# The opening of a routed-attention and tanh-shrink kernel: order of weight fetches, first masks and a later pair's loads

## The chip, the cores and the metric

One core of one Trainium2 chip. The metric is device microseconds of one execution. The kernel before the change takes 991.08 us (median of 3 runs, 991.01 to 991.74). Engine names: TensorE (PE, its weight loads PEld), VectorE (DVE), ScalarE (ACT), GpSimd (POOL, "the pool"), and SyncE (SP), whose queue issues most of the DMAs.

## What is computed

Attention in which a query and a key see each other only if both have the same nearest centroid, and then a two-layer block over the joined heads. Batch 4, 8 heads, 768 positions, 64 channels per head, 16 centroids; the block goes from 512 to 2048 and back.

```python
q_assign = np.argmax(np.einsum('bhsd,hcd->bhsc', q_n, c_n), axis=-1)
k_assign = np.argmax(np.einsum('bhsd,hcd->bhsc', k_n, c_n), axis=-1)
mask = q_assign[:, :, :, None] == k_assign[:, :, None, :]
scores = np.where(mask, scale * np.matmul(q, k.transpose(0, 1, 3, 2)), -1e9)
attn = softmax(scores)                 # over the keys
x = np.matmul(attn, v)                 # heads joined: (3072, 512)
h = x @ w_in
out = (h - np.tanh(h)) @ w_out
```

The two weight matrices arrive as 8-byte floats and are read as pairs of 32-bit words; q, k and v are 4-byte floats.

## The kernel before

**Pairs and steps.** Two heads make a pair, so there are 16 pairs; pairs 0 to 3 (HP is 4) are batch 0. The scores of a pair are made transposed, keys on the partitions, in two halves of 384 queries, and each half in three steps of 256 keys. The list `steps` (L904) has 96 entries (pair, half, step): the first 12 are the first halves of pairs 0 to 3, the next 12 their second halves, then one pair after the other.

**One step.** `begin` (L435) makes the scores on TensorE (L443) and the exponentials on ScalarE (L465). `select` (L467) multiplies a tile of exponentials, on VectorE, by 1 where the key's code equals the query's code, else 0 (L475). It reads the queries' codes from a tile `row`, in which they are spread over all 128 partitions. `value` (L490) multiplies by v on TensorE (av, L497). `sum_up` (L504) adds up the denominators of the first halves on TensorE (den, L511 and L518). The loop from L1031 writes a step's work in this order: what belongs to later pairs, `begin` of the following step, `rest_of` for today's weight pieces, `value`, `sum_up`, then a list `todo` (select of the following step, stages of later pairs, denominators, weight pieces). The order is manual; each engine gets its instructions in the order in which the code writes them.

**Codes.** For each pair, `turn` (L319) transposes q and k (pt, L324; copied out by ScalarE, L331), `similar` (L337) multiplies by the centroids (sim, L343), `route` (L350) finds the best centroid with four VectorE operations (L362 to L369), and `publish` (L383) transposes the codes (pq, L388), copies them (qc, L392) and writes them to DRAM through SP (L394). From there `spread` (L398) loads a `row` (L401). In the first halves of pairs 1 to 3, `masked` (L378), no `select` is needed: `spread_both` (L406) loads the codes of both sides into a tile `hot` (L410), `one_hot` (L414) turns it into the two factors of a mask on VectorE (L418, L422), and `begin` adds the mask to the scores by matmuls (L454).

**Opening.** Lines 980 to 1019 are written out by hand: loads of pair 0 (`load`, L302, four DMAs on SP's queue for q and k, and two for v), constants, the codes of pair 0, its first `row`, the codes of pair 1, and `begin` of the steps 0, 1 and 2. The stages of the later pairs (`before`, L908: turns, similar, route, publish, spread_both, one_hot) are put on steps by a table (L927 to L935); for pair 3 they fall on steps 3, 4, 4, 5, 5 and 7. `turns` of pair 3 also calls `load(4)`, which has no buffer to wait for.

**Weight pieces.** The matrices come in 32 pieces of 512 KB, fetched by the pool's queue (`fetch`, L209, DMA at L217) into three buffers. `rest_of` (L219) makes two ScalarE operations of a piece (L148, L149), into one of two buffers `rest`; `round_piece` (L224) makes two VectorE operations (L157, L160) and then fetches the piece three further on. Pieces are counted from 0 here. Pieces 0 and 1 are done in the opening, where a small pool copy, the gate (L987), holds back the first fetches until pair 0's k has come. The table `paces` (L1028) says how many pieces each step takes.

**Denominators of the first halves.** For pairs 0 and 1, `total`, `compact`, `invert`, `spread_out` and `scale` (L530 to L585) follow at steps +0, +1, +2, +3 and +5 after a half's last step: SP writes a list (L550), loads it compactly (L563, tiles each and other), VectorE adds and inverts (L571, L572), SP writes it back (L574) and spreads it (den<-back, L579), VectorE scales (L585). Pairs 2 and 3 are divided directly (`divide`, L587).

From step 12 on the block of batch 0 fills the gaps (h at L612, o at L628), and later batches use a seven-product scheme (pu at L804, pd at L855).

Of the kernel before, what the change touches and what calls it, by code (L numbers as in the profile page):

```python
# [58 lines left out]
def kernel(  # L59
# [10 lines left out]
    nc = tc.nc  # L70
# [8 lines left out]
    HP = H // 2  # L79
# [98 lines left out]
    def fast():  # L178
# [123 lines left out]
        def load(n: int, what=(0, 1)):  # L302
            if n >= len(pairs):
                return
            b, p = pairs[n]
            for i in what:
                if i < 2:
                    pool, tag = (gp, "g") if b == 0 else (loads, f"x{i}")
                    t = raw_qk[n, i] = pool.tile([P, NCH, 2, D], F32, name=f"x{i}", tag=tag)
                else:  # L310
                    pool = vp0 if n in (2, 3) else vp
                    t = vals[n] = pool.tile([P, 2, NCH, D], F32, name="vals")
                for h in range(2):
                    nc.sync.dma_start(
                        t[:, :, h] if i < 2 else t[:, h],
                        (q, k, v)[i][b, 2 * p + h].rearrange("(p j) d -> p j d", p=P),
                    )

        def turn(n: int, i: int, engine):  # L319

            pt = ps_s.tile([P, 2, 512], F32, name="pt", tag="s")
            x = raw_qk.pop((n, i))
            for j in range(NCH):
                nc.tensor.transpose(  # L324
                    out=pt[:, j // HCH, (j % HCH) * P : (j % HCH + 1) * P],
                    in_=x[:, j].rearrange("p h d -> p (h d)"), identity=ident,
                )
            pool = turnp0 if n in (2, 3) else turnp
            t = turned[n, i] = pool.tile([P, 2, TB], F32, name=f"t{i}")
            if engine is nc.scalar:  # L330
                nc.scalar.copy(out=t, in_=pt[:, :, 0:TB])  # L331
            else:
                nc.vector.tensor_copy(out=t, in_=pt[:, :, 0:TB])
# [3 lines left out]
        def similar(n: int):  # L337

            ps = ps_f.tile([P, TB], F32, name="sim", tag="f")
            for i in range(2):  # L340
                for half in range(2):
                    r = (2 * i + half) * 2 * C
                    nc.tensor.matmul(  # L343
                        ps[r : r + 2 * C], lhsT=bd[:, pairs[n][1]],
                        rhs=turned[n, i][:, half], start=True, stop=True, tile_position=(0, r),
                    )
            sims[n] = rtp.tile([P, TB], F32, name="simt")
            nc.scalar.copy(out=sims[n], in_=ps)
# [25 lines left out]
        def summed(n: int, half: int):  # L374

            return n < HP and half == 0

        def masked(n: int, half: int):  # L378


            return summed(n, half) and n > 0
# [14 lines left out]
        rows, hots = {}, {}  # L396
# [9 lines left out]
        def spread_both(n: int):  # L406

            t = hots[n] = gp.tile([P, 2, 2, TB], BF16, name="hot", tag="g")
            for h in range(2):
                nc.sync.dma_start(  # L410
                    t[h * D : h * D + D], q_codes[n][:, :, h].unsqueeze(0).to_broadcast([D, 2, 2, TB])
                )
# [16 lines left out]
        def weight_tiles(n: int, half: int, s: int):  # L429
            if (n, half, s) == (0, 0, NS - 1):  # L430
                return [gp.tile([P, 2, TB], F32, name="e", tag="g") for _ in range(2)]
            t = ep.tile([P, 2, 2, TB], F32, name="e")
            return [t[:, i] for i in range(2)]

        def begin(step):  # L435
            n, half, s = step
            sc = {}
            for i in range(2):
                j = 2 * s + i
                sc[i] = ps_s.tile([P, 2, 512], F32, name="sc", tag="s")  # L440
                for h in range(2):
                    r = slice(h * D, h * D + D)
                    nc.tensor.matmul(  # L443
                        sc[i][:, h, 0:TB],
                        lhsT=turned[n, 1][r].rearrange("p a n -> p (a n)")[:, j * P : (j + 1) * P],
                        rhs=turned[n, 0][r, half], start=True, stop=not masked(n, half),
                    )
            for i in range(2):
                j = 2 * s + i
                out = sc[i][:, :, 0:TB]  # L450
                if masked(n, half):
                    for h in range(2):
                        r = slice(h * D, h * D + D)
                        nc.tensor.matmul(  # L454
                            sc[i][:, h, 0:TB],
                            lhsT=hots[n][r, 1].rearrange("p a n -> p (a n)")[:, j * P : (j + 1) * P],
                            rhs=hots[n][r, 0, half], start=False, stop=True,
                        )
                if summed(n, half):
                    if i == 0:  # L460
                        weights[n, half, s] = weight_tiles(n, half, s)
                    out = weights[n, half, s][i]
                else:
                    scores[n, half, j] = sc[i]
                nc.scalar.activation(out=out, in_=sc[i][:, :, 0:TB], func=ACT.Exp, scale=SCALE)  # L465

        def select(n: int, half: int, j: int):  # L467

            if not masked(n, half):
                if j % 2 == 0 and not summed(n, half):  # L470
                    weights[n, half, j // 2] = weight_tiles(n, half, j // 2)
                e = weights[n, half, j // 2][j % 2]
                sc = e if summed(n, half) else scores.pop((n, half, j))
                for h in range(2):
                    nc.vector.scalar_tensor_tensor(  # L475
                        out=e[:, h], in0=rows[n, half][:, h],
                        scalar=codes[n][:, 1, j // HCH, h, j % HCH : j % HCH + 1], in1=sc[:, h, 0:TB],
                        op0=ALU.is_equal, op1=ALU.mult,
                    )
            if j % 2 == 1 and not summed(n, half):  # L480
                pair = weights[n, half, j // 2]
                if j == 1:
                    s = sums[n, half] = sump.tile([P, 2, TB], F32, name="sum")
                    nc.gpsimd.tensor_tensor(out=s, in0=pair[0], in1=pair[1], op=ALU.add)  # L484
                else:
                    s = sums[n, half]
                    for i in range(2):
                        nc.gpsimd.tensor_tensor(out=s, in0=s, in1=pair[i], op=ALU.add)  # L488
# [278 lines left out]
        def strassen_items(b: int):  # L767
# [136 lines left out]
        steps = [(p, half, s) for half in range(2) for p in range(HP) for s in range(NS)] + [  # L904
            (n, half, s) for n in range(HP, len(pairs)) for half in range(2) for s in range(NS)
        ]

        def before(n: int):  # L908


            def turns():
                turn(n, 0, nc.scalar)
                turn(n, 1, nc.scalar)
                if n >= HP - 1:
                    load(n + 1)

            yield turns
            yield lambda: similar(n)
            yield lambda: route(n)
            yield lambda: publish(n)  # L920
            if masked(n, 0):
                yield lambda: spread_both(n)
                yield lambda: one_hot(n)


# [60 lines left out]
        gate = const.tile([P, 1], F32, name="gate")  # L986
# [16 lines left out]
        load(2)  # L1003
        rest_of(1)
        begin(steps[0])
        for _ in range(2):
            round_piece(rounding.pop(0))
        route(1)
        begin(steps[1])
        begin(steps[2])  # L1010
        publish(1)
        spread_both(1)
        load(1, (2,))
        load(3)
        for n in range(2, HP):
            load(n, (2,))
        for i in range(2):
            select(*steps[0][:2], i)
        ready[1] = {**ready.get(1, {}), 5: lambda: one_hot(1)}


# [3 lines left out]

        paces = dict(enumerate((0, 0, 1, 2, 0, 0, 2, 2, 1, 1, 1, 0, 3, 2, 2, 2, 2, 2, 2, 3, 2)))  # L1028
        late, divides, makers, later = [], [], [], {}
        fill, whole, spent, since, over = [], 0.0, 0.0, 0, 1  # L1030
        for at, (n, half, s) in enumerate(steps):  # L1031
# [108 lines left out]
        for t, bound in (  # L1140
# [7 lines left out]
            out=fits, in0=inverse, scalar1=MOST_INVERSE * words, scalar2=None, op0=ALU.is_le  # L1148
        )
        nc.vector.scalar_tensor_tensor(  # L1150
            out=fits, in0=inverse, scalar=words / SUM_MOST, in1=fits, op0=ALU.is_ge, op1=ALU.mult
        )
        checks = [fits, largest]
        if words == 2:
            nc.vector.tensor_scalar(
                out=smallest, in0=smallest, scalar1=HIGH_LEAST, scalar2=None, op0=ALU.is_ge
# [161 lines left out]
    with ExitStack() as cx, tc.manual_schedule():  # L1318
        fast()
# [35 lines left out]
```

## Time and profile before

| | value |
|---|---|
| median of 3 runs | 991.08 us |
| span of the profiled execution | 990.3 us (that run: 992.06 us) |
| granted TensorE clock | 0.998 |
| VectorE busy | 531.4 us |
| ScalarE busy | 321.7 us |
| pool busy | 499.7 us |
| DMA moved | 132.47 MB, mean 134 GB/s |

A line of the chain of waits has a start and a duration in us, and what ran: an engine and its line, a DMA, or "issue", time in which the engine waited for nothing that the profile shows. A line of the timeline has a start, a duration, engine, line, operation, written tile <- read tiles, shapes and a count; in brackets stands how long the engine was idle before it and what ended that. "SPq" is SP's queue. Windows give each engine's busy time in a stretch, and what share of the 16 DMA engines was busy.

### The profile page before, as it was taken

How to read it: one execution, taken by the hardware profiler on the slowest of the kernel's cores; microseconds unless marked ns; L12 is line 12 of the kernel's file. 1: busy time of each engine (PE TensorE's matmuls, PEld its weight loads, DVE VectorE, ACT ScalarE, POOL GpSimd, SP SyncE). 2: the span in 40 equal slices, each digit the busy share in tenths (PEclk: the TensorE clock that was granted, in tenths of full speed). 3: DMA queues.
4: the chain of work that ended last, by engine and by line, in shares of the span. 5: the costliest groups of instructions: out<-in, count | busy, mean ns of one | idle time of the engine just before them, and what ended most of it. 6: DMA issues, size and time to landing. Idle time of an engine off the chain costs nothing.

```text
span 990.3 us, 16579 instructions
## 1 busy us (share of the span) xinstructions
PE 976.6 (99%) x6444; PEld 467.0 (47%) x6444; DVE 531.4 (54%) x1017; ACT 321.7 (32%) x493; POOL 499.7 (50%) x346
## 2 busy tenths in 40 slices
PE   7999999999999999999999999999999999999997
PEld 4344443344443334444455555444455555444664
DVE  5547567448655667656554357655645336533011
ACT  5566564233442333343331222324341221122000
POOL 1015334444445464786777345676688345466600
PEclk9999999999999999999999999999999999999999
DMA  8854363125475724463536637344453232233321
GB/s 209 211 136 140 112 181 105 30 51 153 120 217 144 218 91 126 147 173 118 176 111 201 193 117 215 109 148 123 149 166 95 99 110 74 103 112 127 103 102 35
DMA packets 115977, 132.47 MB, mean 134 GB/s; under 512 B 62980, under 2 KB 95668, under 8 KB 113204
## 3 DMA queue, kind: packets, MB, share of 16 engines
q1 hardware_dynamic: 109508, 109.81, 37.3%
q0 software_dynamic: 6240, 21.50, 6.6%
q8 instruction: 53, 0.87, 0.4%
q14 instruction: 32, 0.26, 0.1%
q10 hardware_dynamic: 144, 0.03, 0.0%
HBM read 110.14 MB, written 21.17 MB: 133 GB/s over the span
## 4 chain that ended last, share of the span: by engine, by line
PE 96%; DVE 2%; DMA 1%; ACT 1%; issue 0%; POOL 0%; ACTq 0%; DVEq 0%
PE pd L855 22%; PE pu L804 21%; PE sc L443 14%; PE av L497 14%; PE o L628 8%; PE h L612 8%; PE pt L324 2%; PE den L537 2%; PE sim L343 1%; PE warm L294 1%; PE den L511 1%; DMA row<-q_codes 1%; PE pr L356 1%; DVE e L475 1%; PE den L518 0%
## 5 line engine op out<-in xcount | busy, mean ns | idle before, releaser
L488 POOL TENSOR_TENSOR sum<-sum,e 128x768 f32<-128x768 f32 x112 | 206.1, 1840 | 107.6 <-DVE e L475 103.8
L475 DVE SCALAR_TENSOR_TENSOR e<-row,code,sc 128x384 f32<-128x384 bf16 x336 | 185.2, 607 | 99.1 <-ACT sc L465 77.8
L855 PE MATMUL pd<-stream,G 128*64 128x256 f32 x1728 | 191.8, 379 | 0.0
L465 ACT ACTIVATE sc<-sc 128x768 f32<-128x768 f32 x168 | 125.9, 792 | 202.7 <-PE sc L443 187.9
L855 PEld LDWEIGHTS pd<-stream,G 128*64 128x64 f32 x1728 | 123.8, 137 | 67.4 <-issue 7.9
L443 PE MATMUL sc<-t,t 64*128 64x384 f32 x768 | 150.0, 509 | 0.9 <-ACT e L465 0.9
L497 PE MATMUL av<-e,vals 128*64 128x384 f32 x768 | 145.6, 498 | 1.8 <-DVE e L475 1.8
L799 POOL TENSOR_TENSOR G<-G,th 128x768 f32<-128x768 f32 (+1 forms) x51 | 88.0, 1738 | 98.6 <-ACT th L797 98.6
L804 PE MATMUL pu<-xT,stream 128*64 128x384 f32 x768 | 134.9, 488 | 0.7 <-DVE top L364 0.7
L804 PE MATMUL pu<-diff,stream 128*64 128x384 f32 x576 | 103.1, 487 | 0.0
L443 PEld LDWEIGHTS sc<-t,t 64*128 64x128 f32 x768 | 66.0, 186 | 74.8 <-issue 41.9
L484 POOL TENSOR_TENSOR sum<-e 128x768 f32<-128x768 f32 x28 | 56.8, 2028 | 74.6 <-DVE e L475 66.3
L804 PEld LDWEIGHTS pu<-xT,stream 128*64 128x64 f32 x768 | 54.1, 137 | 69.5 <-issue 62.5
L497 PEld LDWEIGHTS av<-e,vals 128*64 128x64 f32 x768 | 47.6, 136 | 83.1 <-issue 78.9
L612 PE MATMUL h<-xT,w_in 128*64 128x384 f32 x512 | 86.3, 487 | 0.1
L628 PE MATMUL o<-w_out,g 128*64 128x512 f32 x384 | 86.3, 594 | 0.0
L797 ACT ACTIVATE th<-G 128x768 f32<-128x768 f32 (+1 forms) x51 | 40.9, 806 | 117.6 <-DVE G L792 114.0
L804 PEld LDWEIGHTS pu<-diff,stream 128*64 128x64 f32 x576 | 40.8, 137 | 49.9 <-issue 44.5
L792 DVE TENSOR_TENSOR G<-pu,u 128x384 f32<-128x384 f32 x72 | 39.8, 552 | 41.4 <-PE pu L804 41.2
L612 PEld LDWEIGHTS h<-xT,w_in 128*64 128x64 f32 x512 | 36.4, 137 | 46.3 <-issue 44.7
L628 PEld LDWEIGHTS o<-w_out,g 128*64 128x64 f32 x384 | 27.1, 137 | 50.3 <-issue 49.6
L866 DVE SCALAR_TENSOR_TENSOR c<-pd,du 128x256 f32<-128x256 f32 x36 | 15.1, 420 | 62.5 <-PE pd L855 62.5
(123 smaller groups left out, 843.5 us busy)
## 6 DMA issues: line engine op xcount, KB each, us to landing
stream<-up_factors SPq DMA_DIRECT2D x24, 896.0 KB
stream<-down_factors SPq DMA_DIRECT2D x21, 1024.0 KB
raw<-in_moe_w_in_dram POOLq DMA_DIRECT2D x16, 512.0 KB, 5.8
raw<-in_moe_w_out_dram POOLq DMA_DIRECT2D x16, 512.0 KB, 5.2
again<-in_moe_w_in_dram SPq DMA_DIRECT2D x32, 256.0 KB
again<-in_moe_w_out_dram SPq DMA_DIRECT2D x32, 256.0 KB
x<-in_q_dram SPq DMA_DIRECT2D x32, 192.0 KB
x<-in_k_dram SPq DMA_DIRECT2D x32, 192.0 KB
```

Of the source, the lines that this page charges most:

```text
L443: nc.tensor.matmul(sc[i][:, h, 0:TB], lhsT=turned[n, 1][r].rearrange("p a n -> p (a n)")[:, j * P : (j + 1) * P], rhs=turned[n, 0][r, half ...
L465: nc.scalar.activation(out=out, in_=sc[i][:, :, 0:TB], func=ACT.Exp, scale=SCALE)
L475: nc.vector.scalar_tensor_tensor(out=e[:, h], in0=rows[n, half][:, h], scalar=codes[n][:, 1, j // HCH, h, j % HCH : j % HCH + 1], in1=sc[: ...
L484: nc.gpsimd.tensor_tensor(out=s, in0=pair[0], in1=pair[1], op=ALU.add)
L488: nc.gpsimd.tensor_tensor(out=s, in0=s, in1=pair[i], op=ALU.add)
L497: nc.tensor.matmul(avs[n, half][h * D : h * D + D], lhsT=vals[n][:, h, j], rhs=e[i][:, h], start=(j == 0), stop=(j == NCH - 1),)
L612: nc.tensor.matmul(h[r], lhsT=w_in[i][:, c, o * P : (o + 1) * P][:, r], rhs=xT[c][:, half], start=(c == 0), stop=(c == CD - 1),)
L628: nc.tensor.matmul(acc[sub][r], lhsT=gs[f % HF][:, f // HF, sub * P : (sub + 1) * P][:, r], rhs=w_out[f // FQ][:, f % FQ], start=(f == seq ...
L797: nc.scalar.activation(out=th, in_=t, func=ACT.Tanh)
L799: nc.gpsimd.tensor_tensor(out=t, in0=t, in1=th, op=ALU.subtract)
L804: nc.tensor.matmul(ps[r], lhsT=streams[base + i][:, c, k_, r], rhs=right[c], start=(c == 0), stop=(c == CH - 1),)
L855: nc.tensor.matmul(ps[r], lhsT=left(i)[:, r], rhs=t[:, i], start=(i == 0), stop=(i == HF - 1))
```

## The change

Four edits, all to the order of the work; what is computed stays.

```diff
@@ before(n): turns()
-                if n >= HP - 1:
+                if n >= HP:
                     load(n + 1)
@@ before(n)
             if masked(n, 0):
-                yield lambda: spread_both(n)
+
+                def spreads():
+                    spread_both(n)
+                    if n == HP - 1:
+                        load(n + 1)
+
+                yield spreads
                 yield lambda: one_hot(n)
@@ opening
         begin(steps[0])
+
+        nc.gpsimd.tensor_copy(out=gate, in_=rows[0, 0][:, 0, 0:1])
         for _ in range(2):
             round_piece(rounding.pop(0))
         route(1)
         begin(steps[1])
-        begin(steps[2])
+        select(*steps[0][:2], 0)
         publish(1)
         spread_both(1)
+        begin(steps[2])
         load(1, (2,))
         load(3)
         for n in range(2, HP):
             load(n, (2,))
-        for i in range(2):
-            select(*steps[0][:2], i)
+        select(*steps[0][:2], 1)
@@ paces
-        paces = dict(enumerate((0, 0, 1, 2, 0, 0, 2, 2, 1, 1, 1, 0, 3, 2, 2, 2, 2, 2, 2, 3, 2)))
+        paces = dict(enumerate((0, 0, 1, 1, 1, 0, 2, 2, 1, 1, 1, 0, 3, 2, 2, 2, 2, 2, 2, 3, 2)))
```

The load of pair 4's q and k goes from the step of pair 3's turns (step 3) to that of its `spread_both` (step 5). A second gate on the pool reads one element of each partition of the first `row`, ahead of the fetches of pieces 3 and 4 (the fourth and fifth). The first tile of step 0 is selected before the codes of pair 1 are published, and `begin` of step 2 comes after that. Step 3 takes one piece instead of two, and step 4 one instead of none.

## The prediction

> **What bounds the kernel now.** I read the page's busy shares first, then its chain that ended last.
>
> ```profile
> span 990.3 us, 16579 instructions
> PE 976.6 (99%) x6444; PEld 467.0 (47%) x6444; DVE 531.4 (54%) x1017; ACT 321.7 (32%) x493; POOL 499.7 (50%) x346
> PE 96%; DVE 2%; DMA 1%; ACT 1%; issue 0%; POOL 0%; ACTq 0%; DVEq 0%
> ```
>
> TensorE is busy all but 13.7 us, so a change that leaves its work alone wins only idle time. Windows of 25 us place it: 5.4 us idle in 0:25, 1.6 in 25:50, then 25.00 of 25 nearly everywhere (24.66 the lowest), and 5.9 in the last window, at the tail, which the change doesn't touch. So at most the 7.0 us of the opening are to be had. The chain in order of time, in 14:48, shows where they lie:
>
> ```profile
> 17.45 6.42 DMA row<-q_codes
> ...
> 23.96 0.63 DVE e L475
> 24.59 0.04 issue
> 24.63 2.45 PE av L497 x8
> 27.08 0.10 issue
> 27.18 0.85 PE pt L324 x6
> 28.03 0.47 issue
> 28.50 0.85 PE pt L324 x6
> ...
> 43.84 0.65 ACT t L331
> 44.49 0.04 issue
> 44.54 1.54 PE sim L343 x8
> 46.08 1.49 PE sc L443 x8
> ```
>
> Two places matter. First, the row broadcast takes 6.42 us; TensorE waits for the first select until 24.63, and the first eight av matmuls, 1.44 us elsewhere in the chain, take 2.45 at the DVE's pace. Second, sim of pair 3 waits for ScalarE's copy at 43.84, which stands behind two weight pieces. After 46 us nothing idles, but the timeline shows a tight place ahead, in VectorE and ScalarE rows of 61:72:
>
> ```profile
> 61.85 0.55 DVE L585 TENSOR_TENSOR xT<-xT,den 128x384 f32<-128x384 f32 x1
> 66.49 0.17 DVE L571 TENSOR_TENSOR each<-each,other 128x6 f32<-128x6 f32 x1 [4.08 <-DMA other<-list]
> 68.05 0.79 ACT L148 ACTIVATE rest<-raw 128x512 uint16<-128x512 uint32 x1 [0.90 <-DVE w_in L160]
> 70.18 1.51 ACT L465 ACTIVATE e<-sc 128x768 f32<-128x768 f32 x2
> ```
>
> VectorE waits 4.08 us for a small list; rest of piece 9 then waits for piece 7's buffer, and the exponentials of step 10 start at 70.18, right behind. TensorE needs the first of them at 72.96 (the scores of step 11).
>
> [...] 979 KB moved from 18 to 23 us, by the half-microsecond windows, while the row is 192 KB. [...] the second pair's codes, issued from 23.71, behind the 768 KB of pair 2's q and k, let the hot loads start only at 29.21.
>
> **The change part by part.** "Step" is an entry of the list of 96.
>
> *A. Pieces 3 and 4 (from 0) held until the first row has landed; select and publish reordered.* The gate is one pool copy (0.18 us, as the one at L987). Behind it on the pool stand only the two fetches; they were issued at 17.01 and 18.80, their pieces are first used at 41.17 and 42.44, and a fetch takes 4.2 to 8.0 us, so some 17 us of other work hide the wait. The gain is the row's: from 15 to 18 us the DMA is idle, and without 1 MB beside it the row should land sooner. [...] high end 4.74, the two hot loads of pair 1 (29.21 to the end of their wait at 33.95, twice the bytes). I take 3.5: their bytes begin to move 1.7 us after the issue, half of them at 250 GB/s take 0.8, and about 1 us for the end. The row lands at 21.0, before the codes of pair 1 are ready (21.46).
> VectorE: select 0 (two of 0.63) to 22.75, codes copy to 23.05 (before: 23.18), select 1 to 24.3. The copy now stands behind the row; at 21.0 that costs nothing. TensorE: publish's transpose waits for the codes, 21.65 to 21.93; scores of step 2 to 23.5 instead of 22.66 (their move by 0.3 is part of this sum); then av, first half at once, second at select 1's pace, to 24.95 instead of 27.08: 2.1 us. The 0.47 before the second pt, which I read as the wait for pair 2's k, goes too, since 1 MB less precedes it; and the copies are then ahead of sim. The transposes end at 26.8, den at 27.6, sim at 28.45, so the next av starts at 28.45 instead of 31.08: **2.6 us**. It holds on if hot of pair 1 lands by 31.8: the codes are written from 23.1, done by some 25.5, and 4.74 to 6.66 us (pair 2's hot loads, 40.42 to 47.08, beside pieces) give 30.2 to 32.2. Ends for A: 1.4 (a row at 22.5) and 2.7.
>
> *B. One piece instead of two at step 3.* One rest is two activations of 0.63 to 0.68: 1.25 us by the chain. k's copy ends 1.25 earlier, and sc starts at 44.83 instead of 46.08 (TensorE alone could at 43.53 + 0.85 = 44.4): **1.25 us**, ends 0.7 and 1.6. The piece goes to step 4, where ScalarE idles 3.06 us (49.3 to 52.35) and VectorE has 1.1 us between 53.0 and 54.88. Its fetch of piece 7 goes from 44.20 to about 54; piece 7 is used at 62.54. Free.
>
> *C. load(4) moved behind hot of pair 3.* Four issues of 192 KB. Nobody needs them before step 17, so their own move is free, and they leave the crowded 43 to 51 us. But on SP's queue they now stand in front of den<-back (57.88), list<-den (59.18) and the list loads (61.50, 62.89), whose landing ends the 4.08 us wait. Times as before, with the whole opening shifted alike: issues 57.8 to 61, or to about 64 if the last stalls as pair 4's k does (44.78, 4.22 us). 768 KB at 240 GB/s take 3.3 us, and from 61 pieces 8 and 9 (1 MB) share: done between 64.6 and 66.7. Then den<-back (192 KB, about 0.8 us) and the list chain, which lands between 69 and 71 instead of 66.4. VectorE's L571, and with it piece 7, rest of 9 and the exponentials of step 10, come 2.4 to 4.3 us later, say 3.2. The slack is 72.96 - 70.18 - 0.8 = 1.95, so TensorE loses **1.25 us**; ends 0 (the bytes fit in the idle DMA of 53 to 57 and the gaps to 61) and 2.4. The shift cannot help here, since VectorE, ScalarE and TensorE move together.
>
> Sum: 2.6 + 1.25 - 1.25 = **2.6 us**. It is made on the profiled span, 990.3, which becomes 987.7; the timed runs lie at 991.01 to 991.74, 0.8 above it, so 991.08 becomes **988.5**. After 90 us TensorE's windows show no idle over 0.34 us until the tail, so what is won by then lasts.
>
> **The rivals.** *1. C is hidden:* the list lands within the 1.95 us of slack. For it: the DMA is idle in 53:57 and moves 205 GB/s in 58:61, less than the 266 of 31:35. Against: den<-back stands behind 768 KB in one queue. 2.6 + 1.25 = 3.85: 987.2. *2. C takes most back, or A is small:* SP stalls and the pieces go first, C 2.4, and the row lands at 22.5, A 1.4: 0.25 us net, or 1.1 with A at 2.3: about 990.2. *3. The gate finds nothing:* the row took its 6.42 us for itself and not because of the pieces. For it: in 18 to 21 us the DMA moves only 155 GB/s at a share of 0.63, so it was not full. Then select 0 holds up the codes of pair 1 by 1.3 us, A is about 0, and B and C cancel: 991.1. *4. Slower, by the list chain alone:* load(4) in front delays L571 by 8 us, the four issues stalling like 19.13's (4.48) and 44.78's (4.22) one after the other; TensorE then loses 8 - 1.95 = 6.05 at step 11. It decides from a delay of 1.95 + 3.85 = 5.8 us; at 8 it gives 991.08 + 2.2 = 993.3.
>
> **How the numbers follow.** About 0.2% (2 us) is what a measurement of this kernel can tell from no change. Forecast (987.6 to 989.6): 0.48, of which 0.40 lie past 2 us; rival 1: 0.22, all faster; rival 2: 0.17, same; rival 3: 0.06, same, or slower for 0.02; rival 4: 0.07, 0.06 of it slower, 0.01 same. So faster 0.62, same 0.08 + 0.17 + 0.04 + 0.01 = 0.30, slower 0.08. The range, 986.8 to 990.9, takes in the forecast, rival 1 and most of rival 2, and leaves out the last two.
>
> **What would show it.** A: the row lands near 21 us, first av near 23.5, second av near 28.5; wrong if the row still takes 6 us or the codes copy waits for it. B: only one rest between the exponentials and the copies of pair 3, and no idle before sim. C: L571's wait stays but ends later against the step's av; a TensorE wait on ScalarE before the scores of step 11. The prediction falls if the hot loads of pair 1 come after 32 us, or if list<-den issues over 6 us later than the steps around it.

## The result, and the profile after

The changed kernel takes 997.0 us (median of 6 runs, 995.64 to 998.53), against 991.41 for the kernel before in the same series: a ratio of 1.0057, 95% interval 1.0044 to 1.007. It is 5.6 us slower, where 2.6 us faster was forecast. The page of one execution after (995.64 us by its own time, the quickest of the six):

```profile
span 993.9 us, 16587 instructions
PE 977.3 (98%) x6444; PEld 467.4 (47%) x6444; DVE 529.9 (53%) x1017; ACT 321.4 (32%) x493; POOL 499.7 (50%) x347
PE 94%; DVE 2%; DMA 2%; SPq 1%; ACT 0%; issue 0%; POOL 0%; ACTq 0%; DVEq 0%
```

TensorE's work is unchanged (977.3 us busy against 976.6) and its share of the chain has fallen from 96% to 94%: the time is new waiting. SP's queue, absent from the chain before, holds 1% of it. The waits of TensorE alone (who waited for whom, us in total, times, longest):

```profile
PE av L497 <- ACT xT L528: 5.2, 1, 5.2
PE sc L454 <- DVE hot L422: 0.7, 1, 0.7
```

The waits for the first select (1.8) and for pair 3's copies (1.2, now 0.2) are gone or nearly so, as forecast; one of 5.2 us has come in. The chain leads back from it, and here ran through SP's queue for ten microseconds:

```profile
51.81 3.12 DMA q_codes<-qc
...
58.67 3.81 SPq L314
62.48 0.04 issue
62.52 0.73 SPq L579
...
67.17 1.56 DMA other<-list
...
68.82 0.18 DVE each L571
...
71.02 0.75 ACT rest L149
71.77 0.33 ACT xT L528
72.10 0.04 issue
72.15 2.72 PE av L497 x8
74.87 1.78 PE den L511 x8
```

The last of load(4)'s four DMAs (L314) stalls for 3.8 us at SP, den<-back (L579) and the list come behind it, then L571, a rest, the take of pair 2 (L528), and the av of step 9. In the rows of the timeline that answer to those of 61:72 before:

```profile
67.37 0.56 DVE L585 TENSOR_TENSOR xT<-xT,den 128x384 f32<-128x384 f32 x1 [7.05 <-DMA den<-back]
68.82 0.17 DVE L571 TENSOR_TENSOR each<-each,other 128x6 f32<-128x6 f32 x1 [0.89 <-DMA other<-list]
70.38 0.77 ACT L148 ACTIVATE rest<-raw 128x512 uint16<-128x512 uint32 x1 [5.10 <-DVE w_in L160]
```

VectorE now stands 7.05 us at den<-back, where it did not wait before, and ScalarE 5.10 us in front of rest of piece 9, where it stood 0.90. One more cost stands in two windows (stretch and its length, busy us and count of PE, PEld, DVE, ACT and POOL, then the granted clock, the DMA share and GB/s):

```profile
66.00:72.00 6.00, 0.92 (x8) 0.20 (x4) 3.29 (x9) 1.62 (x4) 1.48 (x2) 1.00 0.17 20
72.00:77.00 5.00, 4.85 (x19) 1.86 (x20) 4.04 (x6) 3.29 (x6) 2.18 (x3) 0.66 0.89 264
```

After five idle microseconds the clock is 0.66 on average; the av takes 2.72 us instead of 1.44, the den 1.78 instead of 1.29. The place costs 5.2 + 1.3 + 0.5 = 7.0 us, and eats twice over the 3.4 us won earlier (the av of step 8 began at 65.69 before and begins at 62.30 now). This execution is the mildest of the six: its granted clock is 0.997 over the whole span, that of the other five 0.995, and they took 0.7 to 2.9 us more; 0.002 of 994 us is about 2 us, an estimate from these clocks of what the difference is worth; where in those executions it lay, no trace here shows.

### The profile page after: what moved, and what is told of

It is laid out like the page before. It is cut to its first block, busy times and chain, and to the rows that moved or that the text cites. A ratio compares the mean times of both kernels' runs of the same rounds, so it can differ in the third digit from the quotient of the medians.

```text
span 993.9 us, 16587 instructions
## 1 busy us (share of the span) xinstructions
PE 977.3 (98%) x6444; PEld 467.4 (47%) x6444; DVE 529.9 (53%) x1017; ACT 321.4 (32%) x493; POOL 499.7 (50%) x347
## 4 chain that ended last, share of the span: by engine, by line
PE 94%; DVE 2%; DMA 2%; SPq 1%; ACT 0%; issue 0%; POOL 0%; ACTq 0%; DVEq 0%
PE pd L855 22%; PE pu L804 21%; PE av L497 13%; PE sc L443 13%; PE o L628 8%; PE h L612 8%; PE pt L324 2%; PE den L537 2%; PE sim L343 1%; PE warm L294 1%; DMA q_codes<-qc 1%; SPq L314 1%; PE pr L356 1%; DVE e L475 1%; PE den L511 0%; DMA hot<-q_codes 0%
```

## The experiments

Ratios are to the kernel before in the same series (medians 991.6 to 992.0), with 95% intervals. Single executions differ by over 1 us in when the first codes are ready (the first row is issued between 16.30 and 17.65 us), so the sizes are read from the timed ratios, and the profiles for who waits for whom and for times against TensorE's own steps.

**Theory:** load(4), moved to step 5, stands in front of den<-back and the list loads on SP's queue, and delays TensorE by way of VectorE, rest of piece 9 and the take. **Rival 1:** the weight pieces that are held or moved come late. **Rival 2:** load(4)'s bytes slow pieces 8 and 9.

### The load back in its place

```diff
-                if n >= HP:
+                if n >= HP - 1:
                     load(n + 1)
...
-                    if n == HP - 1:
-                        load(n + 1)
```

> The changed kernel with load(4) back in the turns of pair 3, all else as changed. Theory (the load in front of the list chain on SP's queue delays VectorE, rest of piece 9 and the take of pair 2, and TensorE waits for the one av buffer): the wait of 5.2 us before av and the slow matmuls behind it vanish, and what A and B won stays: 3.5 us under the kernel before, about 987.8. Rival 1 (the held and moved pieces are to blame, because pieces 7 to 9 come later): the loss stays, 995 or more.

Measured: 990.57 us, ratio 0.9989 (0.9981 to 0.9997). The loss is gone, so it was this edit's; against 1.0057 with it, the edit costs 0.68% or 6.7 us there. But only 1.1 of the 3.4 us are kept, where all of it was expected. TensorE's waits say where the rest went, to hot of pair 1 (1.0) and of pair 3 (0.4), and again to the take:

```profile
PE sc L454 <- DVE hot L422: 1.4, 2, 1.0
PE av L497 <- ACT xT L528: 1.2, 1, 1.2
```

and SP's queue with the pool's gives a second reason for a late list:

```profile
50.21 0.53 POOL L217 DMA_DIRECT2D raw<-in_moe_w_in_dram  x1 [9.52 <-ACT e L465]
...
51.22 0.31 SPq L394 DMA_DIRECT2D q_codes<-qc  x1
54.62 1.27 SPq L410 DMA_DIRECT2D hot<-q_codes  x2
```

Piece 7, which is fetched where piece 4 is rounded, now goes out at 50.21, one microsecond ahead of the codes of pair 3. These take until 54.6 to land, 3.4 us after their issue; before, 1.3 (55.19 to 56.51). What stands behind them on SP's queue comes late; and the list (L550), which took 2.3 us from its first issue to its first load before (59.18 to 61.50), takes 5.3 beside pieces 8 and 9 (57.29 to 62.62). So rival 1 holds in part, but not as it was put: piece 7 is not missed itself, it holds up a small transfer.

### The load alone

```diff
 (the kernel before)
-                if n >= HP - 1:
+                if n >= HP:
                     load(n + 1)
...
+                    if n == HP - 1:
+                        load(n + 1)
```

> The kernel before with load(4) behind hot of pair 3, and no other edit. Theory: TensorE stalls before the av of step 9 for some 5 us and runs slowly after it, 6 to 8 us in all: about 998. Rival 1: no loss, 991. My prediction's own price for this edit: 1.25 us, 992.3.

Measured: 995.48 us, ratio 1.0046 (1.0033 to 1.006). Slower by itself, but by 4.6 us (the medians differ by 3.7, the two profiled spans by 3.4), less than expected:

```profile
PE av L497 <- ACT xT L528: 3.0, 1, 3.0
```

The wait is the same and shorter, and behind it the av takes 1.51 us and the clock stays at 1.00. Without A and B there is no shift and no late codes to add to the delay. SP's stall is missing too: the last of the four issues took 1.04 us instead of 3.81. Three of the four issues were over by 60.25, and piece 8 is fetched near 59.9 (an estimate: 59.70 in the kernel before, whose av of step 8 begins 0.2 us earlier than here); in the changed kernel piece 8 went out together with the first of them, at 56.31.

### The load in step 6 and in step 12

```diff
-                    if n == HP - 1:
-                        load(n + 1)
...
+            if at == 6:          # the other kernel: 12
+                todo.append(lambda: load(HP))
```

> The changed kernel with load(4) at the end of step 6, so that on SP's queue it stands behind den<-back, list<-den and the two list loads instead of in front of them; its bytes still move at the time of pieces 8 and 9. Theory (order on the queue): no wait of TensorE over 1 us in 50:80, about 988. Rival 2 (the bytes beside pieces 8 and 9 are what costs): pieces 8 and 9 land late, ScalarE waits 2 us or more for them, and half of the loss or more stays: 993 or more.

> The changed kernel with load(4) at the end of step 12, where the DMA of the kernel before is idle (82 to 92 us). Theory and rival 2 alike: no stall, about 987.5, some tenths under the run with the load back in the turns if the crowded 43 to 50 us mattered for TensorE. Rival 1: 995.

Measured: 990.2 and 990.49 us, both ratios 0.9989 (0.9981 and 0.998 to 0.9997). Both are as good as with the load in the turns, but 2 to 3 us short of what was expected, and both keep a wait of 1.1 to 1.2 us for the take, which comes from piece 7 as above. In step 6 the loads went out at 62.89, when pieces 8 and 9 had passed, so this run can't tell the place on the queue from the bytes. Against rival 2 stands that ScalarE waited 1.96 us for piece 8 in the changed kernel and 2.07 in the one with the load back. With the load alone it did wait 1.61 us for piece 8, where it had not before, but TensorE had no wait behind that.

### A alone and B alone

```diff
 (the kernel before; A)
+        nc.gpsimd.tensor_copy(out=gate, in_=rows[0, 0][:, 0, 0:1])
...
-        begin(steps[2])
+        select(*steps[0][:2], 0)
         publish(1)
         spread_both(1)
+        begin(steps[2])
...
 (the kernel before; B)
-        paces = dict(enumerate((0, 0, 1, 2, 0, 0, ...
+        paces = dict(enumerate((0, 0, 1, 1, 1, 0, ...
```

> The kernel before with the gate and the new order of select, publish and begin; paces and load(4) as before. Theory (piece 4's round moved to step 4 sends the fetch of piece 7 beside the codes of pair 3, and that alone brought the list chain late in the run with the load back in the turns): the codes of pair 3 land in under 2 us, no TensorE wait of 1 us before the av of step 9, and the whole 2.6 us of A stay: 989.0. Rival 1 (TensorE ahead by 2.6 us outruns the chain in any case): 1 us or more is lost at step 9, 990 or more.

> The kernel before with only the two entries of paces changed. Theory: TensorE wins 1.2 us before sim of pair 3 and loses 1 to 2 us before the av of step 9, because the codes of pair 3 take 3 us to land beside piece 7: 991 to 992, no gain. My prediction's price for this edit: 990.2.

Measured: A 989.95 us, ratio 0.9982 (0.9975 to 0.9989); B 991.29 us, 1.0004 (0.9996 to 1.0013). A wins 1.8 of the 2.6 us; no wait is left at step 9, so being ahead does no harm by itself, and rival 1's form of it falls. What A loses is in its opening:

```profile
22.52 5.14 DMA q_codes<-qc
...
28.35 4.35 DMA hot<-q_codes
```

The codes of pair 1 need 5.14 us, since pieces 3 and 4 start at 21.11, as soon as the row is in. B wins 1.0 us at sim (1.2 of wait became 0.2) and loses 0.9 in a wait for the take at step 9: nothing remains. (The codes of pair 3 took 3.1 us there, 52.90 to 56.00.)

### The two halves of A

> The kernel before with only the gate on the first row; select, publish and begin in the old order, paces and load(4) as before. Theory: the row lands near 21 and the first select starts as soon as route is done (21.5), av by some 22.9; then the hot loads of pair 1, held up by the codes that land beside pieces 3 and 4, take back 1 to 1.6 us: about 990.2, most of what A alone gave. Rival (the row's time is its own): 991.5.

> The kernel before with only the new order of select, publish and begin in the opening, no gate; paces and load(4) as before. Theory: the row still lands near 23.9; the codes of pair 1 now wait for it behind the select, 1.3 to 2 us later than before, and the scores of step 2 move into the idle time; hot of pair 1 comes later, and TensorE waits for it: 991.5 to 994. Rival (the order is what A won by): 989.5 to 990.

Each is a part of the edit A shown above. Gate alone: 990.32 us, ratio 0.9984 (0.9977 to 0.999), which can't be told from A whole. Order alone: 991.29 us, 0.9996 (0.9988 to 1.0004), no change; a little better than expected. There the row takes 6.4 us again (issued at 16.30, first select at 22.70), VectorE waits 2.38 of them at the select, and the codes go out 1.5 us later after the row's issue than before; yet hot goes out 11.7 us after it, as in the kernel before (11.8), since the codes land late in either case. With the gate the row landed in 3.3 us (A alone: 17.23 to 20.56). So some 3 of its 6.42 us were the pieces' doing, and the prediction's rival 3 falls.

### Where the delay reaches TensorE

```diff
 (the changed kernel; first: rest of piece 9 behind the take)
+            if at != 8:
                 for piece in todays[:2]:
                     rest_of(piece)
...
+            if at == 8:
+                for piece in todays[:2]:
+                    rest_of(piece)
...
 (the changed kernel; second: piece 9 in step 9)
-        (0, 0, 1, 1, 1, 0, 2, 2, 1, 1, ...
+        (0, 0, 1, 1, 1, 0, 2, 2, 0, 2, ...
```

> The changed kernel, load(4) in step 5 and all, with rest of piece 9 behind the take of pair 2 on ScalarE instead of ahead of it. Theory (TensorE's first wait is for the one av buffer, which the take frees): no wait before the av of step 9; the exponentials of step 10 are still held until 72.4, so TensorE waits some 3.8 us at the scores of step 11 instead of 5.2 plus a slow clock: 993.5 to 995.5. Rival (the av buffer doesn't matter, the exponentials of step 10 set the wait): no change, 997.

> The changed kernel, load(4) in step 5 and all, with piece 9 taken in step 9 instead of step 8, so that no rest waits on ScalarE in front of the take of pair 2 and of the exponentials of step 10. Theory (the delay reaches TensorE only through that place): the 5.2 us wait before av and the slow clock behind it vanish although the list still lands 6 us late; 988 to 991. Rival (the delay reaches TensorE by another way, for instance den of pair 2 on VectorE): 994 or more.

Measured: 992.35 us, ratio 1.0012 (1.0001 to 1.0022), and 993.11, 1.002 (1.0011 to 1.0028). With the take ahead, 0.45% of the 0.57% are gone, more than expected; the av of step 9 no longer waits, and the next wait is the one that I had priced:

```profile
72.14 2.40 PE L443 MATMUL sc<-t,t 64*128 64x384 f32 x8 [3.10 <-ACT e L465]
```

With piece 9 in step 9 less came back than expected (988 to 991): that rest no longer holds the take, but piece 10, fetched when VectorE got to piece 7, kept ScalarE waiting 3.38 us, and TensorE 2.8. The late list has several ways to TensorE, and the take was the first.

### A version that is faster than both

First, B without its fetch: paces as before, but rest of piece 4 behind pair 3's copies on ScalarE, A as it is, the load in step 12.

```diff
+            first_rests = todays[: 1 if at == 3 else 2]
+            for piece in first_rests:
                 rest_of(piece)
...
                     stages.pop(0)()
+                for piece in todays[len(first_rests) : 2]:
+                    rest_of(piece)
                 sum_up(n, half, s)
```

> A as in the change; paces as before, but in step 3 ScalarE does rest of piece 4 behind the copies of pair 3's turns instead of ahead of them, so that piece 7 is still fetched in step 3; load(4) at the end of step 12. Theory: A and B both stay, 3.6 to 3.9 us under the kernel before, about 987.9, and no TensorE wait in 50:80. Rival 1: 990, as the other runs without the load in step 5.

Measured: 988.6 us, ratio 0.9972 (0.9962 to 0.9983). The codes of pair 3 land in time again, and 50:75 is full:

```profile
51.19 0.31 SPq L394 DMA_DIRECT2D q_codes<-qc  x1
52.52 1.24 SPq L410 DMA_DIRECT2D hot<-q_codes  x2
```

A wait of 1.2 us for hot of pair 1 is left. So, second, the gate moves from the first row to that tile:

```diff
 (on top of the last)
-        nc.gpsimd.tensor_copy(out=gate, in_=rows[0, 0][:, 0, 0:1])
         for _ in range(2):
-            round_piece(rounding.pop(0))
+            round_piece(rounding.pop(0), False)     # without its fetch
...
         spread_both(1)
+        nc.gpsimd.tensor_copy(out=gate, in_=hots[1][:, 0, 1, 0:1])
+        for i in range(2):
+            fetch(AHEAD + i)
         begin(steps[2])
```

> The run with rest behind the turns, with pieces 3 and 4 held until the hot tile of pair 1 has landed instead of the first row. Theory (the codes of pair 1 land 4.5 us after their issue because pieces 3 and 4 start beside them): the codes land in 2 us, the wait of 1.2 us before the mask matmuls of step 3 goes, and v of pair 1 and x of pair 3, now beside the pieces, still come in time: 987.4 to 988. Rival (the codes wait for the end of pair 2's k, whatever the pool fetches): no change, 988.6; or v of pair 1 comes late and it is worse.

Measured: 988.09 us, ratio 0.9961 (0.9948 to 0.9973), 3.9 us under the kernel before and the fastest seen. Its queue (lines are one further down in this kernel) and the windows of TensorE:

```profile
22.63 0.32 SPq L395 DMA_DIRECT2D q_codes<-qc  x1
25.19 1.28 SPq L411 DMA_DIRECT2D hot<-q_codes  x2
```

```profile
0.00:25.00 25.00, 20.89 (x107) 13.10 (x108) 16.59 (x63) 13.22 (x19) 2.57 (x10) 1.00 0.73 184
25.00:50.00 25.00, 25.00 (x181) 10.52 (x179) 12.18 (x27) 14.77 (x23) 3.26 (x6) 1.00 0.76 216
50.00:75.00 25.00, 25.00 (x157) 10.84 (x155) 13.24 (x25) 18.66 (x28) 6.22 (x9) 1.00 0.64 181
```

The codes of pair 1 land 2.6 us after their issue instead of 5.1 as with A alone, and from 25 to 75 us TensorE doesn't idle. The intervals of the last two runs overlap; that the second is the faster rests on the trace more than on the times.

## Why the prediction was wrong

**The step that failed is C**, "so TensorE loses 1.25 us; ends 0 and 2.4". It measured 6.7 us in the changed kernel and 4.6 alone. The path was the one described up to rest of piece 9; its last link was another, and three parts of the sum were wrong. The prediction's own signs of failure came: list<-den went out at 64.77 instead of 59.18, 9.0 us later against the steps around it, and the hot loads of pair 1 landed at 32.2, just past 32. The fourth rival had the direction; that its 6.05 us lie near the measured loss is luck, since its delay (8 us) and its slack (1.95) were both off.

- *The slack.* "72.96 - 70.18 - 0.8 = 1.95" took the exponentials of step 10 for the first thing that TensorE needs. Before them on ScalarE stands the take of pair 2, which frees the one av buffer (the pool `ps_a` has one), and the av of step 9 needs it: before, the take ended at 69.78 and the av began at 70.23, a slack of 0.45. The run with the take ahead shows both: no wait at the av, then one at the scores. In the timeline before (the first line is the av of step 8):

```profile
65.69 1.51 PE L497 MATMUL av<-e,vals 128*64 128x384 f32 x8
...
69.33 0.45 ACT L528 COPY xT<-av 128x384 f32<-128x384 f32 x1
...
70.23 1.51 PE L497 MATMUL av<-e,vals 128*64 128x384 f32 x8
```

- *The delay.* "2.4 to 4.3 us later, say 3.2". With the load alone L571 came at 70.19, 3.5 us late against TensorE's steps (its av of step 8 began at 65.88): inside the range, and 3.5 - 0.45 is the wait of 3.0. So for the load by itself only the slack was wrong. In the changed kernel L571 came at 68.82, where the shift of 3.4 us would have put it at 63.1: 5.7 late, and 5.7 - 0.45 is the wait of 5.2. Some 1.7 of it are not the load's but piece 7's, which B had sent in front of the codes of pair 3: in the run with the load back, where the codes lost 2.1 us to it (3.4 against 1.3), L571 still came at 64.83.
- *The clock.* The sum had no term for what follows a long wait: 1.8 us at a lower clock, after 5.2 us of idling. Behind the 3.0 us of the load alone the trace has none of it.

**B was right in its gain and wrong in "Free".** Most of the 1.25 us at sim came (1.2 of wait became 0.2), but the fetch that goes with the moved piece was priced only for the piece's own use, 8 us later, and not for the small write that is issued 1 us behind it. Alone, B is worth nothing.

**A was right in its mechanism and mis-sized.** The row landed in 3.3 to 3.8 us instead of 6.42 (3.5 was taken, with 1 us of it, for the end, an estimate of mine that no trace showed), the first av began at 23.38 (near 23.5) and the second at 28.06 (near 28.5). The term that was off is "done by some 25.5" for the codes of pair 1: they landed at 27.4 in the changed kernel, and TensorE waited for hot. The prediction read the late codes of the kernel before as standing behind the 768 KB of pair 2's q and k; in the last run, with the same loads ahead of them but no pieces beside them, they took 2.6 us. Its 979 KB between 18 and 23 us did not show that the pieces slow the row either, since those 768 KB were issued from 17.84 on; the gate does (3.3 us with it, 6.42 without). Alone A gave 1.8 us.

**"The shift cannot help here, since VectorE, ScalarE and TensorE move together"** holds only as long as DMA chains start as early. With the two small writes kept clear of the pieces, the whole 2.6 + 1.25 us are there, with the gate in another place than A's: 3.9 us in the last run.

All three places (the row, the codes of pair 1 and those of pair 3) look alike: a small transfer on SP's queue takes longer when pieces from the pool's queue are under way. The row took 6.42 us beside pieces 3 and 4 and 3.3 with A alone, where they were held. The 6 KB of codes took, from their issue to that of the first hot load, 1.3 us for pair 3 in the kernel before and 2.6 for pair 1 in the last run, both with no piece under way; beside one or two pieces they took 3.2 for pair 3 in the changed kernel (51.81 to 55.00, piece 7 issued at 50.74) and 5.2 for pair 1 with A alone (22.52 to 27.68, pieces 3 and 4 issued from 21.11). By what way the pieces hold them up, no trace here shows.

## What to carry to other kernels

A load that nobody needs soon still has a place on its queue: before it is moved, list what is issued behind it there, down to the last small transfer, and follow each to the first instruction that waits, buffers included. Moving a piece of work moves what it triggers (here the fetch three pieces on); look what small, urgent transfer is issued within the next microseconds. And an idle time of several microseconds on TensorE can cost more than itself: 5.2 us of waiting cost 7.0 here.

## What was not expected of the hardware

The granted clock was 0.50 for 3.4 us after TensorE waits of 5.2 us (changed kernel), 3.1 (take ahead) and 2.8 (piece 9 in step 9), but stayed at 1.00 after 3.0 (load alone) and 1.2. In the run with the take ahead:

```profile
70.00:73.00 3.00, 0.86 (x4) 0.46 (x6) 1.88 (x4) 2.79 (x5) 2.35 (x4) 0.95 0.71 169
73.00:76.00 3.00, 3.00 (x14) 1.20 (x14) 2.97 (x5) 1.21 (x2) 0.76 (x2) 0.50 0.97 279
```

So near 3 us it isn't the length of the wait alone that decides; what else does, these runs do not show. By windows of 0.1 us the half clock lasted from 72.3 to 75.7 in the changed kernel. In the other two the times are estimates from the clock in windows of 1 us: 72.7 to 76.1 in this one (0.86 in 72:73, 0.93 in 76:77), and 77.2 to 80.6 with piece 9 in step 9 (0.58 in 77:78, 0.71 in 80:81). The length is the same each time, but it began 0.6 us after TensorE's return (72.14) here and 0.1 us ahead of it (77.28) there. Half clock for 3.4 us is 1.7 us of work lost, against the 1.8 read from the av and den above. SP's issue of a DMA also stalled, for 3.81 us (from 58.67, changed kernel), with pieces 8 and 9 issued at 56.31 and 57.62; why it does so was not tried.
